# First attention's transposes into the second product's PSUM banks, and the second attention five pieces later

## The chip, the cores and the metric

The kernel runs on one core of a Trainium2 chip. The metric is the time of one execution on the device in microseconds (us); lower is better. Times are medians of several executions; a profile is one further execution with the hardware profiler on. The engines are PE (TensorE: matmuls and transposes), DVE (VectorE), ACT (ScalarE), POOL (GpSimd) and SP, whose queue issues nearly all DMAs. Each engine works through its own instructions in order.

## The reference

Attention with a causal window of 128 and a distance bias, then a two-layer product with the mish function, all in float32 (the two weight matrices arrive as float64):

```python
scores = q @ k.T / sqrt(64) + bias;  allowed where 0 <= i - j < 128   # batch 8, heads 8, seq 576, head 64
attn = softmax(scores);  x = attn @ v              # x becomes 4608 tokens x 512
h = x @ w_in                                       # 512 -> 2048
out = (h * tanh(softplus(h))) @ w_out              # 2048 -> 512
```

## The kernel before

The program is unrolled Python; every engine executes its instructions in program order, and that order is written out by hand: each piece of work is a pair (time, function), the lists are sorted by time (`run`, L536), and the numbers count units of attention or pieces of the product, not microseconds.

**Batches.** The 576 tokens of a batch are done as 512 and a remainder of 64; the remainders of all batches are the ninth round. Round `c` has a first product (`first`, L450: eight `j` of 24 matmuls) with `mish`, and a second product (`second`, L507: 32 pieces of six matmuls, number `2m + t`). While round `c` does its second product, the attention of batch `c + 1` is mixed into it. Attention of batch 0 has nothing to hide behind: it is the early stage, done with `attention(0, 0.27)` (L559).

**A unit of attention** (`unit`, L247) is two query blocks for a pair of heads; eight units `k` per batch, `p, half = divmod(k, 2)`. Its steps are: `scores` on PE into a PSUM tile `s` of two banks (two such tiles exist); `exps` (DVE takes bias and maximum, ACT the exponent); `fold` (POOL folds the exponents, DVE takes the reciprocals `r`, kept in the second bank of `s`); `scale` (DVE); `weights` (four PE transposes into the first bank of the same `s`, then one DVE multiplication by the masks back into `pz`); `values` (PE, into the one bank `o`); and for odd units `split_x` (ACT and DVE split `o` into a rounded and a remaining part, tile `x`). Even units also carry a `last_unit` (L356) for the 64 left-over tokens.

In the early stage `busy` (L549) adds two groups of four small matmuls per unit that write to unused columns of the second bank of `s` of the unit before: one group just after the next unit's scores, one just after the transposes.

**Converting the weights** (`convert_w`, L134). Each of the 16 weight pieces arrives as float64 bits in two halves and goes through `scaled` (ACT, to a temporary `t`), `joined` (three DVE bit operations, the first into a temporary `u`), `upper` (ACT) and `lower` (a subtraction). With `banks` given, `t` and `u` lie in PSUM banks and POOL does `lower`; with `None`, `t` is a slot of the SBUF ring `gg` (three slots, shared with `parts`), `u` is written over the input in SBUF, and DVE does `lower`. Pieces 0 and 1 are converted in the early stage, 2 to 11 during the first product of round 0, 12 to 15 (the last four of `w_out`, `Co4` to `Co7` below, needed from pieces 8, 10, 12 and 14 on) during the second product of round 0. The matmuls of the second product write to the banks `po0` and `po1`, which are unused in the early stage but for the first two conversions.

`parts` (L475) splits mish's result for the second product: ACT rounds, POOL subtracts, into a slot of `gg`; it runs two products `m` ahead.

Of the kernel before, what the change touches and what calls it, by code (L numbers as in the profile page):

```python
# [8 lines left out]
F32 = mybir.dt.float32  # L9
# [7 lines left out]
P = 128  # L17
# [18 lines left out]
def attention_mish_mlp(  # L36
# [35 lines left out]
    ps = ctx.enter_context(tc.tile_pool(name="ps", bufs=1, space=bass.MemoryType.PSUM))  # L72
# [17 lines left out]
    for t in vb:  # L90
# [3 lines left out]
    pe, dve, act, pool, sp = (  # L94
        InOrder(tc, e) for e in (nc.tensor, nc.vector, nc.scalar, nc.gpsimd, nc.sync)
    )
# [7 lines left out]
    def big(name, dtype):  # L104
        return wts.tile([P, 2048], dtype, tag="w", name=name, bufs=2 * NJ + NF // 4)
# [25 lines left out]
            else:  # L131
                load(t[:, :512].bitcast(F32).rearrange("p (c n) -> p c n", n=n), part)

    def convert_w(kind, j, banks):  # L134

        halves = raw_w.pop((kind, j))
        st = {}

        def value(a):
            return halves[a][:, 1::2].bitcast(F32) if bits else halves[a][:, :512].bitcast(F32)

        def place(a, part):
            return split[(kind, j)][:, 1024 * a + 512 * part : 1024 * a + 512 * part + 512]

        def scaled(a):  # L150
            if a == 0:
                split[(kind, j)] = big(f"s{kind}{j}", F32R)
            if not bits:
                return
            if banks:
                st[a] = ps.tile([P, 512], F32, tag=banks[a][0], name=f"t{kind}{j}_{a}")
            else:
                if a == 0:
                    st["t"] = ff.tile([P, 1024], F32, tag="gg", name=f"t{kind}{j}", bufs=3)
                st[a] = st["t"][:, 512 * a : 512 * (a + 1)]  # L160

            act.activation(st[a], value(a), AF.Copy, scale=2.0**-112)

        def joined(a):
            if not bits:
                return
            low, high, tb = halves[a][:, 0::2], halves[a][:, 1::2], st[a].bitcast(U32)
            u = high
            if banks:
                u = ps.tile([P, 512], F32, tag=banks[a][1], name=f"u{kind}{j}_{a}").bitcast(U32)  # L170
            dve.tensor_scalar(out=u, in0=tb, scalar1=3, scalar2=None, op0=ALU.logical_shift_left)
            dve.scalar_tensor_tensor(
                out=high, in0=low, scalar=29, in1=u, op0=ALU.logical_shift_right, op1=ALU.bitwise_or,
            )
            dve.scalar_tensor_tensor(
                out=high, in0=tb, scalar=0x80000000, in1=high, op0=ALU.bitwise_and,
                op1=ALU.bitwise_or,
            )

        def upper(a):  # L180
            act.activation(place(a, 0), value(a), AF.Copy)

        def lower(a):
            (pool if banks else dve).tensor_tensor(
                out=place(a, 1), in0=value(a), in1=place(a, 0).bitcast(F32), op=ALU.subtract
            )

        return scaled, joined, upper, lower
# [37 lines left out]
    def load_pair(b, p):  # L226
        hs = slice(2 * p, 2 * p + 2)
        qk = at.tile([P, 2, S], F32, tag="qk", name=f"qk{b}_{p}")
        load(qk[:, 0, :], qT[b, hs].rearrange("h d s -> (h d) s"))
        load(qk[:, 1, :], kT[b, hs].rearrange("h d s -> (h d) s"))  # L230
        z = qd[p % 2]
        for i in range(2):
            r = slice(i * D, (i + 1) * D)
            load(z[r, r], qT[b, 2 * p + i, :, CH:S])
        qkv[(b, p)] = (qk, z)
# [11 lines left out]
    def unit(b, p, half, lag):  # L247
# [6 lines left out]
        st = {}  # L254
        blocks = (0, 1) if half == 0 else (2, 3)
        name = f"{b}_{p}_{half}"
# [52 lines left out]

        def weights():  # L310
            pz = st["pz"]

            pt = st["s"][:, 0, :].rearrange("p (c n) -> p c n", c=4)
            for c in range(4):
                pe.transpose(pt[:, c, :], pz[:, c, :P], ident)
            dve.tensor_tensor(
                out=pz.rearrange("p c (u n) -> p u c n", u=2),
                in0=pt.rearrange("p (u c) n -> p u c n", u=1).to_broadcast([P, 2, 4, P]),
                in1=masks.rearrange("p u (c n) -> p u c n", c=1).to_broadcast([P, 2, 4, P]),
                op=ALU.mult,  # L320
            )
# [20 lines left out]
        def split_x():  # L342
# [7 lines left out]

        return [
            (0, scores), (0.02, lambda: exps(0)), (0.25, lambda: exps(1)), (0.7, fold), (0.95, scale),
            (1.3, weights), (1.99 + lag, values), (2.02 + lag, split_x),
        ]

    def last_unit(b, p, lag):  # L356
# [61 lines left out]
    def attention(b, lag=0.0):  # L418

        steps = []
        for k in range(2 * NP):
            p, half = divmod(k, 2)
            for u in [unit(b, p, half, lag)] + ([last_unit(b, p, lag)] if half == 0 else []):
                steps += [(k + d, f) for d, f in u]
            if half:
                nxt = (b, p + 2) if p + 2 < NP else (b + 1, p + 2 - NP)
                if 0 < nxt[0] < B:  # L430
                    steps.append((k + 0.03, lambda nxt=nxt: load_pair(*nxt)))
                    steps.append((k + 2.01, lambda nxt=nxt: load_v(*nxt)))
        return sorted(steps, key=lambda s: s[0])
# [16 lines left out]
    def first(c, j, blocks=range(NCC)):  # L450
        if blocks[0] == 0:
            hs[j % 2] = ps.tile([P, 2, CH], F32, tag="s", name=f"h{c}_{j}", bufs=2)
        h = hs[j % 2]
        for t, cc in (
            [(t, cc) for cc in blocks for t in range(2)] if len(blocks) < NCC
            else [(t, cc) for t in range(2) for cc in blocks]
        ):
            x = xt[(c, cc)]
            for k, (w_, x_) in enumerate(((0, 0), (0, 1), (1, 0))):
                pe.matmul(  # L460
                    h[:, t, :], lhsT=w_part("i", j, w_, cc)[:, t * P : (t + 1) * P],
                    rhs=x[:, x_, :], start=(cc == 0 and k == 0), stop=(cc == NCC - 1 and k == 2),
                )
# [20 lines left out]
    po = {}  # L484
# [51 lines left out]
    def run(steps):  # L536
        for _, work in sorted(steps, key=lambda s: s[0]):
            work()

    def converting(weights, times, banks):  # L540

        steps = []
        for (kind, j), at_ in zip(weights, times):
            st = []
            steps.append((at_[0], lambda kind=kind, j=j, st=st: st.extend(convert_w(kind, j, banks))))
            steps += [(t, lambda n=n, st=st: st[n // 2](n % 2)) for n, t in enumerate(at_)]
        return steps

    def busy(n, place):  # L549
        for _ in range(n):  # L550
# [6 lines left out]


    early = attention(0, 0.27) + converting(  # L559
        conv[:2],  # L560
        [
            (4.1, 4.6, 4.45, 4.97, 4.8, 5.3, 4.82, 5.32),
            (5.6, 6.1, 5.97, 6.45, 6.3, 6.8, 6.32, 6.82),
        ],
        (("po0", "po1"), ("po0", "po1")),
    )
    for k in range(2 * NP):
        if k:
# [2 lines left out]
    early += [  # L571
        (8.6, lambda: first(0, 0, (0,))),
        (9.3, lambda: first(0, 0, (1, 2))),
        (9.31, lambda: first(0, 0, (3,))),
    ]
    busy(18, ps.tile([P, 512], F32, tag="po0", name="idle")[:, : 2 * P])
    run(early)
# [1 line left out]
    for c in range(B + 1):  # L579

        steps = []
        for j in range(NJ):
            if c or j:
                steps.append((j, lambda j=j: first(c, j)))
            steps.append((j + 0.9, lambda j=j: mish(c, j)))
        steps += [(NJ - 1.05, lambda j=j: parts(c, 0, j)) for j in range(2)]
        if c == 0:
            steps += converting(
                conv[2:12],
                [  # L590
                    [-0.5 + 0.84 * n + d for d in (0, 0.42, 0.3, 0.72, 0.75, 1.15, 0.8, 1.2)]
                    for n in range(10)
                ],
                (("po0", "w"), ("po1", "o")),
            )
        run(steps)
        if c == 0:
            load_w(*last_w)

        n = 4 * NJ  # L600
        steps = []
        for m in range(2 * NJ):
            for t in range(2):
                steps.append((2 * m + t, lambda m=m, t=t: second(c, *divmod(m, NJ), t)))
            if m >= 2:
                steps.append((2 * m - 4.1, lambda m=m: parts(c, *divmod(m, NJ))))
        if c == 0:
            steps += converting(
                conv[12:],
                [  # L610
                    [0.3 + 2.5 * n + d for d in (0, 0.6, 0.8, 1.4, 1.7, 2.2, 2.0, 2.5)]
                    for n in range(4)
                ],
                None,
            )
        if c + 1 < B:
            steps += [((n - 2) / 9.0 * s - 0.2, f) for s, f in attention(c + 1)]
        elif c + 1 == B:
            steps.append((4.5, last_x))
        run(steps)  # L620
# [63 lines left out]
```

## Time and profile before

| | us |
|---|---|
| median of 3 runs | 1052.24 (1049.55 to 1052.77) |
| profiled execution | 1053.68 |
| its span, first to last instruction | 1051.9 |
| mean granted TensorE clock | 0.982 of full speed |
| PE busy in the span | 1008.9 (96%) |
| DVE, ACT, POOL busy | 367.1, 395.6, 293.4 |

The profiled execution lies 1.78 us above its span and 1.44 us above the median. Busy PE time counts matmuls at either clock, so a full row of PE is not yet PE at its best; the stages have to be looked at one by one.

### The profile page before, as it was taken

What the parts mean: (1) busy time and instruction counts of PE and PEld (TensorE: products, weight loads), DVE (VectorE), ACT (ScalarE), POOL (GpSimd) and SP (SyncE); (2) the same over time, 40 slices, a digit from 0 to 9 for tenths busy, and PEclk for the clock granted to TensorE, in tenths of its full rate; (3) what the DMA queues carried; (4) which work ended last, traced back from release to release, by engine and by line L of the source; (5) the groups of instructions that cost most, each with busy time, mean ns of one, the idle gap of its engine ahead of it and who ended that gap; (6) DMA issues with size and microseconds to landing.
All of it is one profiled execution on the core that took longest, in us unless ns stands there. A gap on an engine that the chain in (4) does not pass through costs nothing.

```text
span 1051.9 us, 14258 instructions
## 1 busy us (share of the span) xinstructions
PE 1008.9 (96%) x5358; PEld 793.8 (75%) x5358; DVE 367.1 (35%) x1118; ACT 395.6 (38%) x958; POOL 293.4 (28%) x286
## 2 busy tenths in 40 slices
PE   7579969999999999999999999999999999999998
PEld 4348747787778877887788777877787778888886
DVE  4659796402550065005520463026401650010000
ACT  3437744314442354225421543145324542231121
POOL 2215633203330244004410432033302440141042
PEclk9869988999999999999999999999999999999999
DMA  8940111200220023002210032003100201010001
GB/s 271 398 173 1 64 37 57 69 1 25 72 61 30 1 62 93 33 1 61 68 59 1 26 94 68 1 26 93 55 15 5 69 24 41 1 41 21 1 0 41
DMA packets 52133, 59.32 MB, mean 56 GB/s; under 512 B 13024, under 2 KB 32608, under 8 KB 52064
## 3 DMA queue, kind: packets, MB, share of 16 engines
q1 hardware_dynamic: 50880, 57.69, 17.1%
q8 instruction: 42, 0.69, 0.3%
q10 hardware_dynamic: 1184, 0.72, 0.2%
q14 instruction: 27, 0.22, 0.1%
HBM read 47.91 MB, written 10.49 MB: 56 GB/s over the span
## 4 chain that ended last, share of the span: by engine, by line
PE 88%; DVE 3%; ACT 1%; issue 1%; POOL 1%; ACTq 0%; DVEq 0%; POOLq 0%
PE h L30 37%; PE po L30 37%; PE s L30 9%; PE o L30 5%; DVE wo L30 1%; DVE pz L30 1%; ACT pz L30 0%; POOL gg L30 0%; PE pt_3l L30 0%; ACT so L30 0%; DVE so L30 0%; POOL so L30 0%; PE pt_2l L30 0%; PE pt_1l L30 0%; ACT gg L30 0%
## 5 line engine op out<-in xcount | busy, mean ns | idle before, releaser
L30 PE MATMUL po<-so,gg 128*128 128x512 f32 x1728 | 433.2, 401 | 0.0
L30 PE MATMUL h<-x,si 128*128 128x512 f32 x1728 | 394.6, 390 | 0.0
L30 PEld LDWEIGHTS h<-x,si 128*128 128x128 f32 x1728 | 325.0, 188 | 67.7 <-issue 0.2
L30 POOL TENSOR_TENSOR gg<-g,gg 128x512 fp32r<-128x512 f32 x144 | 185.8, 1294 | 671.9 <-ACT gg L30 570.3
L30 PEld LDWEIGHTS po<-so,gg 128*128 128x128 f32 x1728 | 317.6, 190 | 73.3 <-issue 5.7
L30 DVE CUSTOM_DVE_ANT_0 pz<-s,nb 128x256 f32<-128x256 f32 (+1 forms) x256 | 84.6, 387 | 300.9 <-PE s L30 300.8
L30 ACT ACTIVATE g<-h 128x1024 f32<-128x1024 f32 x72 | 73.9, 1027 | 269.1 <-PE h L30 269.1
L30 ACT ACTIVATE pz<-pz,mx 128x256 f32<-128x256 f32 (+1 forms) x256 | 120.4, 471 | 138.4 <-DVE mx L30 138.4
L30 ACT ACTIVATE gg<-g 128x512 fp32r<-128x512 f32 x144 | 88.5, 621 | 48.2 <-PE po L30 46.7
L30 DVE TENSOR_TENSOR pz<-s,masks 128x1024 f32<-128x1024 f32 x64 | 78.2, 1222 | 23.8 <-PE s L30 23.8
L30 POOL TENSOR_TENSOR pz<-pz 128x256 f32<-128x256 f32 x64 | 65.6, 1025 | 29.4 <-ACT pz L30 19.2
L30 DVE TENSOR_TENSOR pz<-pz,s 128x512 f32<-128x512 f32 x64 | 43.8, 684 | 83.9 <-POOL pz L30 83.5
L30 PE MATMUL s<-qk 64*128 64x128 f32 (+1 forms) x448 | 57.7, 376 | 0.0
L30 PE MATMUL o<-pz,va 128*64 128x128 f32 (+1 forms) x560 | 54.9, 325 | 1.6 <-DVE pz L30 1.5
L30 PEld LDWEIGHTS o<-pz,va 128*64 128x64 f32 x560 | 33.3, 136 | 29.7 <-issue 12.0
L30 DVE COPY ob<-po 128x512 f32<-128x512 f32 x18 | 12.4, 691 | 117.4 <-PE po L30 117.4
L30 PE MATMUL s<-ident,pz 128*128 128x128 f32 x256 | 41.2, 286 | 10.6 <-DVE pz L30 9.2
L30 ACT ACTIVATION_READ_ACCUMULATOR pz<-pz,mx 128x1 f32 x256 | 47.8, 187 | 0.0
L30 PEld LDWEIGHTS s<-ident,pz 128*128 128x128 f32 x256 | 32.4, 146 | 20.2 <-DVE pz L30 6.0
L30 ACT ACTIVATE x<-o 128x512 fp32r<-128x512 f32 x32 | 18.8, 587 | 65.0 <-PE o L30 64.6
L30 DVE TENSOR_TENSOR x<-o,x 128x512 fp32r<-128x512 f32 x32 | 22.1, 692 | 59.0 <-ACT x L30 59.0
L30 PEld LDWEIGHTS s<-qk 64*128 64x128 f32 x448 | 33.9, 186 | 11.2 <-issue 8.2
(117 smaller groups left out, 471.8 us busy)
## 6 DMA issues: line engine op xcount, KB each, us to landing
wi<-in_moe_w_in_dram SPq DMA_DIRECT2D x16, 512.0 KB, 10.6
wo<-in_moe_w_out_dram SPq DMA_DIRECT2D x16, 512.0 KB, 10.2
out_dram<-ob SPq DMA_DIRECT2D x32, 256.0 KB, 2.0
qk<-in_q_dram SPq DMA_DIRECT2D x28, 288.0 KB, 3.5
qk<-in_k_dram SPq DMA_DIRECT2D x28, 288.0 KB, 3.8
va<-in_v_dram SPq DMA_DIRECT2D x28, 256.0 KB, 2.8
first<-in_q_dram SPq DMA_DIRECT2D x4, 288.0 KB, 3.8
first<-in_k_dram SPq DMA_DIRECT2D x4, 288.0 KB, 4.3
```

What stands on the lines that cost most here:

```text
L30: return self.tc.keep_in_program_order(method(*args, **kwargs))
```

## The change

- In batch 0, the four transposes of a unit go to a tile in bank `po0` or `po1` (by `half`) instead of the unit's own `s`.
- The first two conversions, which had these banks, use the SBUF ring `gg` instead (with `None`), start one unit earlier, and keep POOL for `lower` (a new argument `last` names that engine).
- `split_x` of batch 0 moves from unit time 2.29 to 2.45, that is from ahead of the masks' multiplication to behind it; the last part of the first product of round 0 moves from 9.31 to 9.5, behind it.
- In the second product of round 0, the four conversions start 0.6 of a piece earlier and follow each other every 2.0 pieces instead of 2.5; the attention of batch 1 begins five pieces later and takes 25/9 pieces a unit instead of 30/9, so that it ends at the same piece. Later rounds keep their times.

```diff
-    def convert_w(kind, j, banks):
+    def convert_w(kind, j, banks, last=pool):
...
         def lower(a):
-            (pool if banks else dve).tensor_tensor(
+            last.tensor_tensor(
                 out=place(a, 1), in0=value(a), in1=place(a, 0).bitcast(F32), op=ALU.subtract
             )
...
         def weights():
             pz = st["pz"]
-
-            pt = st["s"][:, 0, :].rearrange("p (c n) -> p c n", c=4)
+            if b == 0:
+                pt = ps.tile([P, 4, P], F32, tag=f"po{half}", name=f"pt{name}")
+            else:
+
+                pt = st["s"][:, 0, :].rearrange("p (c n) -> p c n", c=4)
             for c in range(4):
                 pe.transpose(pt[:, c, :], pz[:, c, :P], ident)
...
-            (1.3, weights), (1.99 + lag, values), (2.02 + lag, split_x),
+            (1.3, weights), (1.99 + lag, values), (2.45 if lag else 2.02, split_x),
...
-    def converting(weights, times, banks):
+    def converting(weights, times, banks, last=pool):
...
-            (4.1, 4.6, 4.45, 4.97, 4.8, 5.3, 4.82, 5.32),
-            (5.6, 6.1, 5.97, 6.45, 6.3, 6.8, 6.32, 6.82),
+            (3.1, 3.6, 3.47, 3.97, 3.8, 4.3, 3.82, 4.32),
+            (4.6, 5.1, 4.97, 5.47, 5.3, 5.8, 5.32, 5.82),
         ],
-        (("po0", "po1"), ("po0", "po1")),
+        None, pool,
     )
...
-        (9.31, lambda: first(0, 0, (3,))),
+        (9.5, lambda: first(0, 0, (3,))),
...
-                    [0.3 + 2.5 * n + d for d in (0, 0.6, 0.8, 1.4, 1.7, 2.2, 2.0, 2.5)]
+                    [-0.3 + 2.0 * n + d for d in (0, 0.4, 0.7, 1.5, 1.5, 2.4, 1.9, 2.6)]
                     for n in range(4)
                 ],
-                None,
+                None, dve,
             )
         if c + 1 < B:
-            steps += [((n - 2) / 9.0 * s - 0.2, f) for s, f in attention(c + 1)]
+
+            t0 = 0 if c else 5
+            steps += [(t0 + (n - 2 - t0) / 9.0 * s - 0.2, f) for s, f in attention(c + 1)]
```

## Rows read from the trace of the kernel before

**Rows 1.** The page's slices of PE: busy tenths in 40 slices of the span.

```profile
PE   7579969999999999999999999999999999999998
```

**Rows 2.** Windows (early stage; second product, round 0): length, busy by engine, clock, DMA.

```profile
7.00:81.00 74.00, 51.21 (x312) 35.23 (x313) 45.90 (x141) 27.49 (x92) 14.20 (x16) 0.84 0.78 278
119.20:205.70 86.50, 73.88 (x421) 55.33 (x421) 61.55 (x162) 42.38 (x115) 34.02 (x30) 0.92 0.21 63
```

**Rows 3.** Waits of PE from 9.8 to 75 us: total, times, longest.

```profile
PE s L30 <- DVE pz L30: 22.5, 11, 4.6
```

**Rows 4.** Timeline of PE, early stage: start, length, instruction [idle before, releaser].

```profile
24.21 0.60 PE L30 MATMUL s<-masks 128*128 128x256 bf16 x4 [1.32 <-DVE pz L30]
26.57 1.09 PE L30 MATMUL o<-pz,first 128*64 128x128 f32 x12
27.59 0.66 PE L30 MATMUL s<-ident,pz 128*128 128x128 f32 x4
...
30.97 1.00 PE L30 MATMUL s<-masks 128*128 128x256 bf16 x4 [2.73 <-DVE pz L30]
...
48.82 1.01 PE L30 MATMUL s<-masks 128*128 128x256 bf16 x4 [4.64 <-DVE pz L30]
...
75.77 1.09 PE L30 MATMUL o<-pz,first 128*64 128x128 f32 x12
```

**Rows 5.** Timeline of DVE, early stage: masks' multiplication of unit 1, scales of units 1, 2, 3, 7.

```profile
18.96 0.69 DVE L30 TENSOR_TENSOR pz<-pz,s 128x512 f32<-128x512 f32 x1
22.93 1.23 DVE L30 TENSOR_TENSOR pz<-s,masks 128x1024 f32<-128x1024 f32 x1 [0.35 <-PE s L30]
25.32 0.67 DVE L30 TENSOR_TENSOR pz<-pz,s 128x512 f32<-128x512 f32 x1
...
33.05 0.69 DVE L30 TENSOR_TENSOR pz<-pz,s 128x512 f32<-128x512 f32 x1
...
69.12 0.69 DVE L30 TENSOR_TENSOR pz<-pz,s 128x512 f32<-128x512 f32 x1
```

**Rows 6.** Lines by form, DVE, 10 to 73 us: busy, mean ns; a joining operation with PSUM temporaries.

```profile
L30 DVE SCALAR_TENSOR_TENSOR wi<-wi,ui 128x512 uint32<-128x512 uint32 x4 | 2.8, 688 | 0.1
```

**Rows 7.** The weight load that is issued fourth (piece 1, second half), and its landing.

```profile
L30 SPq DMA_DIRECT2D wi<-in_moe_w_in_dram x1: 467/467/467, 18.2 to 18.2; - x1
...
DMA to landing us min/median/max: 8.1/8.1/8.1
```

**Rows 8.** Timeline of PE, second product of round 0.

```profile
134.46 1.11 PE L30 MATMUL s<-ident,pz 128*128 128x128 f32 x4 [5.56 <-DVE pz L30]
135.44 5.22 PE L30 MATMUL po<-so,gg 128*128 128x512 f32 x12
...
146.97 3.00 PE L30 MATMUL po<-so,gg 128*128 128x512 f32 x12
```

**Rows 9.** Lines by form, DVE, 119 to 166 us: busy, mean ns | idle before.

```profile
L30 DVE SCALAR_TENSOR_TENSOR wo<-to,wo 128x512 uint32<-128x512 uint32 x10 | 8.3, 830 | 0.3
L30 DVE TENSOR_TENSOR so<-wo,so 128x512 fp32r<-128x512 f32 x8 | 8.0, 1020 | 2.6 <-ACT so L30 2.6
L30 DVE SCALAR_TENSOR_TENSOR wo<-wo 128x512 uint32<-128x512 uint32 x8 | 6.5, 816 | 0.3
L30 DVE CUSTOM_DVE_ANT_0 pz<-s,nb 128x256 f32<-128x256 f32 x12 | 4.6, 418 | 0.0
L30 DVE TENSOR_SCALAR wo<-to 128x512 uint32<-128x512 uint32 x8 | 4.3, 532 | 3.7 <-ACT to L30 3.7
```

**Rows 10.** Timeline, second product of round 0: ACT's last `upper` of `Co3`; DVE's longest joining.

```profile
122.19 0.66 ACT L30 ACTIVATE so<-wo 128x512 fp32r<-128x512 f32 x1
...
153.02 1.66 DVE L30 SCALAR_TENSOR_TENSOR wo<-wo 128x512 uint32<-128x512 uint32 x1
```

**Rows 11.** Timeline of PE: second product of round 1 begins, and the next first product.

```profile
249.34 0.93 PE L30 MATMUL s<-qk 64*128 64x128 f32 x8
...
316.96 8.32 PE L30 MATMUL h<-x,si 128*128 128x512 f32 x36
```

More of the change, by code (lines that the diff above doesn't have):

```diff
@@ L544, in converting @@
             st = []
-            steps.append((at_[0], lambda kind=kind, j=j, st=st: st.extend(convert_w(kind, j, banks))))
+            steps.append((at_[0], lambda kind=kind, j=j, st=st: st.extend(convert_w(kind, j, banks, last))))
             steps += [(t, lambda n=n, st=st: st[n // 2](n % 2)) for n, t in enumerate(at_)]
```

## The prediction

> **What bounds the kernel now.** I read the page's slices first, 40 of 26.3 us each: PE stands at 9 or more tenths from the seventh slice to the last but one [rows 1], so PE bounds the kernel there, and what does not let PE run sooner or denser elsewhere is worth nothing. The lean slices are the first three and the sixth, the two stretches that the change touches. The windows give their sizes [rows 2]. In the early stage PE is busy 51.2 of 74 us at a granted clock of 0.84; in the second product of round 0 it is busy 73.9 of 86.5 at 0.92. The same second product in round 1, with the same attention but no conversions, takes 316.96 - 249.34 = 67.6 us [rows 11]. So 18.9 us are at stake there, and about 23 of idle in the early stage. Between the two lies the first product of round 0, from the values of unit 7 at 75.77 [rows 4] to 119.2; PE is dense there and the change only shifts it.
>
> In the early stage all of PE's large waits are for DVE: 22.5 us in eleven waits [rows 3]. The timeline tells them apart [rows 4]. Three stand before the first `busy` group of a unit, which needs the reciprocals read by `scale`. Eight stand before the second group, behind the transposes: 1.32 at 24.21 (five such), 2.73 at 30.97, 4.64 at 48.82, one of 2.50. They end when DVE's multiplication by the masks ends: 22.93 + 1.23 = 24.16 [rows 5]. It reads the transposes out of the very `s` that `busy` writes, and the next scores of that `s` stand behind. That is a loop through PE and DVE, once per unit.
>
> In the second product the largest wait, 5.56 us, is that of the transposes of unit 0 for `scale` at 134.46 [rows 8]; DVE is full with conversions there.
>
> **The change, part by part.** *Transposes in `po0`/`po1`.* The eight waits for the masks leave their place. PE goes on to the next scores and next waits for `scale`. How long a unit then takes: from the end of one `scale`, PE does `busy` 0.60, values 1.09, transposes 0.66 [rows 4], DVE the masks 1.23, and then the small work up to the end of the next `scale`, 25.99 - 24.16 = 1.83 [rows 5]: 5.4 us. The scores and exponents of the next unit fit beside this, since the scores are now ahead of it. The other half of a pair has the subtraction of `split_x` where this one has the left-over unit's score; I take the same 5.4. Before, the six units from the end of scale 1 (19.65) to that of scale 7 (69.81) took 50.2 [rows 5]. After: 6 x 5.4 = 32.4, plus the four halves of conversions, which lie in the loop: with SBUF temporaries the means are 0.532 + 0.816 + 0.830 = 2.18 each [rows 9], 8.7 together, against 3 x 0.69 = 2.1 with PSUM ones [rows 6]. Then the clock. Rows 4 show `busy` at 0.60 at full rate (24.21), but 1.00 and 1.01 (1.2 instead of 2.4 GHz) after PE had idled 2.73 and 4.64. Where a conversion lengthens a unit, PE still idles that long for `scale`; at the ratio 1.01/0.60 the 2.35 us of PE in a unit become 4.0. Bounds: no unit slowed, 0; all six, 9.9. I take three, the ones with most conversion: 5.0. Together 46.1 instead of 50.2: -4.1. Ahead of it the first wait of this kind, 1.3, is gone, and behind it the last, 1.3 (the matmuls of the first product then wait for nothing). Early stage: -6.7, between -1.8 and -11.7.
>
> *Conversions a unit earlier.* ACT asks for piece 0 at about 25 us instead of 36. The fourth load lands at 18.2 + 8.1 = 26.3 [rows 7], and piece 1 is asked for a unit and a half later: no wait. POOL's subtractions keep their count.
>
> *`split_x` behind the masks.* Nothing, as PE needs the masks first and `o` is written again only a unit later; without that cover it would be its 0.69 in a pair. The moved quarter of the first product follows it and is in order.
>
> *Second attention five pieces later.* It issues the same instructions. Its load of the pair after next moves with it on SP, behind the last halves of the weights, which it does not pass; it is needed three units later, so it is hidden. The table load before the first exponent no longer stands ahead of `Co4`, while nothing else of ACT is late for it. What counts is when `scale` of unit 0 is done, since PE's transposes wait for it and all pieces stand behind them. PE reaches them after nine pieces at 1.5 (3.00 for two [rows 8]) and three groups of scores near 0.9 [rows 11]: 119.2 + 16.2 = 135.4. DVE has, ahead of that `scale`, all joinings and three weights' subtractions. It begins when ACT has left `Co3` (122.85 [rows 10]) and scaled one half, 123.5; eight halves x 2.18 = 17.4, six subtractions x 1.02 = 6.1, four exponents' maxima at 0.42 at most, 1.4, and the small work 1.83 up to `scale` [rows 5, 9]: 150.2. So PE stands for some 15 us in one wait, where before it stood in several. Behind it lie 67.6 - 16.2 = 51.4 of dense PE [rows 11]. To this come the clock after the idling, as before (5.22 against 3.00 for two pieces [rows 8]), 2.2, and smaller waits. Those were 86.5 - 73.9 - 5.6 = 7.0 [rows 2, 8]; the conversions are gone by then, so I take half, 3.5, with 0 and 7 as ends. End: 207.3 instead of 205.7, +1.6.
>
> Joining with both operands in SBUF: Rows 6 show 0.688 with the temporary in PSUM, rows 9 means of 0.816 and 0.830 with it in SBUF, and rows 10 one of 1.66. The Trainium skill ("SBUF — State Buffer", section "Who interferes with whom") says that a DVE instruction with two SBUF inputs and a POOL instruction that reads SBUF exclude each other, the later one blocking fully; the stretched rows agree. By it alone, each joining that meets POOL would pay like the longest row, which is the third rival below; by the means the sum stands.
>
> **Sum.** -6.7 + 1.6 = -5.1. On the profiled execution, 1053.7, that is 1048.6; the median lies 1.4 below it, so 1047.
>
> **Rivals.**
> *Clock stays low.* All six early units run at 1.2 GHz, because `busy` does not fill the waits for `scale`: the early stage gives only 1.8. For it: 0.84 of the clock over the stage. Against: the waits that went were the ones before the slow rows. -1.8 + 1.6: 1052, no change. The change then does nothing that can be seen, though the waits moved.
> *Second product gains too.* POOL has fewer instructions beside the conversions once the attention is late. Joinings at 3 x 0.69 and subtractions at 0.69 give 123.5 + 16.5 + 4.1 + 3.2 = 147.3; without small waits and slow clock the end is 198.7, -7.0, together -13.7: 1038.5. The true case may lie part of the way.
> *DVE holds the second attention back (slower).* If every two-operand joining is as long as the longest, 1.66, a half costs 3.85, `scale` of unit 0 ends at 123.5 + 30.8 + 9.3 = 163.6, the stage at 220.7, +15: together +8.3, 1060.5. The change is even when that `scale` ends at 155.3, and slower by 0.3% from 158.5 on. Against: only one joining in eight halves was that long.
>
> **How the numbers follow.** This kernel's runs spread by 0.3%, about 3.2 us, which is what can be told from no change. Forecast 0.62 (1042 to 1051: early -4 to -9, second -3 to +5); low clock 0.18; second product gains 0.12; slower 0.08. Faster by over 0.3% (below 1049): most of the forecast, 0.54, the gaining case 0.12, and a little of the low clock: 0.69. Within: 0.22. Slower: 0.09. The range from 1040.5 to 1052.5 leaves out the slower case, half of the gaining one and the edges.
>
> **What would show it.** In the early stage PE's waits before `s<-masks` are only those for `scale`, and no `busy` group starts at the end of a masks' multiplication; scale 1 to scale 7 in 44 to 48 us; the first product of round 0 shifted earlier by 5 to 9. In round 0's second product: no idle PE in the first nine pieces beyond small ones, one wait of 12 to 16 us before the first transposes, and the next first product 85 to 91 us after the first piece. Wrong if `busy` still waits for the masks, if ACT waits for a weight or for a slot of `gg`, or if `scale` of unit 0 ends more than 37 us after the stage's start (155.3 - 119.2 = 36.1).

## The result and the profile after

The changed kernel takes 1045.44 us (median of 5 runs, 1043.91 to 1047.03) against 1052.24 for the kernel before in the same series (1049.55 to 1053.75). The ratio is 0.9938, with a 95% interval of 0.9924 to 0.9952: by the ratio, 6.5 us or 0.6% faster. The profiled execution took 1047.03, with a span of 1045.3.

The two windows of [rows 2], cut at the same events, come first. The columns are length, busy time by engine, granted clock and DMA.

```profile
7.00:71.30 64.30, 47.39 (x313) 33.48 (x314) 46.21 (x141) 27.95 (x92) 14.43 (x16) 0.84 0.91 320
109.60:199.10 89.50, 71.06 (x421) 52.35 (x422) 61.09 (x161) 42.33 (x115) 31.96 (x30) 0.92 0.19 61
```

The early stage is 9.7 us shorter than in [rows 2], at the same mean clock. The second product is 3.0 us longer. PE has the same instructions and 3.8 and 2.8 us less busy time in the two stages, so fewer of them ran at the low clock. The mean clock counts PE's idle time too: from 134 to 139 us, where PE does nothing, it reads 0.50.

PE's waits in the early stage, to be laid beside [rows 3], and the rows of PE's timeline that answer to [rows 4]:

```profile
PE s L30 <- DVE pz L30: 15.0, 6, 4.9
PE o L30 <- issue: 1.7, 1, 1.7
```

```profile
66.04 1.09 PE L30 MATMUL o<-pz,first 128*64 128x128 f32 x12
```

Eleven waits of 22.5 us have become six of 15.0, and each of the six ends with a `scale`; no `busy` group starts at the end of a multiplication by the masks any more. The values of unit 7 start at 66.04 instead of 75.77.

What the second `busy` group held up shows in DVE's rows of a left-over unit, first before and then after the change. In PE's queue the left-over unit's transpose stood behind `busy`, and DVE, with its next `scale` still to come, waited 1.3 us for it, in each of the four even units. That wait is gone.

```profile
32.22 0.42 DVE L30 TENSOR_TENSOR pf_1l<-pt_1l,masks 128x256 f32<-128x256 f32 x1 [1.31 <-PE pt_1l L30]
```

```profile
26.70 0.41 DVE L30 TENSOR_TENSOR pf_1l<-pt_1l,masks 128x256 f32<-128x256 f32 x1
```

DVE's rows for [rows 5], the scales of units 1, 2 and 3 and those of 4 to 7:

```profile
17.20 0.69 DVE L30 TENSOR_TENSOR pz<-pz,s 128x512 f32<-128x512 f32 x1 [0.69 <-POOL pz L30]
...
22.59 0.67 DVE L30 TENSOR_TENSOR pz<-pz,s 128x512 f32<-128x512 f32 x1
...
29.90 0.69 DVE L30 TENSOR_TENSOR pz<-pz,s 128x512 f32<-128x512 f32 x1
...
38.06 0.69 DVE L30 TENSOR_TENSOR pz<-pz,s 128x512 f32<-128x512 f32 x1 [1.13 <-POOL pz L30]
...
48.56 0.69 DVE L30 TENSOR_TENSOR pz<-pz,s 128x512 f32<-128x512 f32 x1
...
55.69 0.67 DVE L30 TENSOR_TENSOR pz<-pz,s 128x512 f32<-128x512 f32 x1
...
61.21 0.69 DVE L30 TENSOR_TENSOR pz<-pz,s 128x512 f32<-128x512 f32 x1
```

From scale to scale that is 5.4, 7.3, 8.2, 10.5, 7.1 and 5.5 us, 44.0 in all. The two units without conversions or cold clock, the first and the last, take 5.4 and 5.5; the prediction built 5.4 from single rows.

In the second product, PE's timeline (for [rows 8]):

```profile
109.65 1.62 PE L30 MATMUL po<-so,gg 128*128 128x512 f32 x6
111.61 5.74 PE L30 MATMUL po<-so,gg 128*128 128x512 f32 x24 [0.34 <-DVE wo L30]
...
125.37 1.19 PE L30 MATMUL po<-so,gg 128*128 128x512 f32 x4 [1.03 <-ACT gg L30]
127.05 0.73 PE L30 MATMUL po<-so,gg 128*128 128x512 f32 x2 [0.49 <-POOL gg L30]
141.40 1.09 PE L30 MATMUL s<-ident,pz 128*128 128x128 f32 x4 [13.61 <-DVE pz L30]
...
199.07 1.29 PE L30 MATMUL h<-x,si 128*128 128x512 f32 x5
```

One wait of 13.61 us has taken the place of the several of before. What DVE did up to it shows in its groups from 109.6 to 150 us, which answer to [rows 9], and in four rows of its timeline: the first operation of `Co4`, two subtractions of the conversions that wait for ACT, and the `scale` of unit 0.

```profile
L30 DVE TENSOR_TENSOR so<-wo,so 128x512 fp32r<-128x512 f32 x8 | 8.3, 1036 | 3.6 <-ACT so L30 3.5
L30 DVE SCALAR_TENSOR_TENSOR wo<-wo 128x512 uint32<-128x512 uint32 x8 | 6.5, 815 | 0.3
L30 DVE SCALAR_TENSOR_TENSOR wo<-to,wo 128x512 uint32<-128x512 uint32 x9 | 6.2, 693 | 0.3
L30 DVE TENSOR_SCALAR wo<-to 128x512 uint32<-128x512 uint32 x8 | 4.6, 569 | 2.1 <-ACT to L30 2.1
```

```profile
113.70 1.09 DVE L30 TENSOR_SCALAR wo<-to 128x512 uint32<-128x512 uint32 x1 [2.14 <-ACT to L30]
...
120.32 1.34 DVE L30 TENSOR_TENSOR so<-wo,so 128x512 fp32r<-128x512 f32 x1 [0.71 <-ACT so L30]
...
134.67 1.32 DVE L30 TENSOR_TENSOR so<-wo,so 128x512 fp32r<-128x512 f32 x1 [1.55 <-ACT so L30]
...
140.58 0.67 DVE L30 TENSOR_TENSOR pz<-pz,s 128x512 f32<-128x512 f32 x1
```

### The profile page after: what moved, and what is told of

Same layout as the page of the kernel before. It is cut to its first block, busy times and chain, and to the rows that moved or that the text cites. A ratio compares the mean times of both kernels' runs of the same rounds, so it can differ in the third digit from the quotient of the medians.

```text
span 1045.3 us, 14263 instructions
## 1 busy us (share of the span) xinstructions
PE 1002.5 (96%) x5358; PEld 789.3 (76%) x5358; DVE 367.0 (35%) x1118; ACT 395.9 (38%) x958; POOL 292.0 (28%) x286
## 4 chain that ended last, share of the span: by engine, by line
PE 83%; DVE 1%; ACT 1%; POOL 0%; issue 0%; POOLq 0%
PE po L30 36%; PE h L30 33%; PE s L30 8%; PE o L30 4%; DVE pz L30 0%; POOL gg L30 0%; PE pt_1l L30 0%; PE pt_2l L30 0%; PE pt_3l L30 0%; PE pt_0l L30 0%; ACT pz L30 0%; POOL pz L30 0%; ACT gg L30 0%; ACT x L30 0%; ACT pz_3l L30 0%
## 5 line engine op out<-in xcount | busy, mean ns | idle before, releaser
L30 DVE TENSOR_TENSOR pz<-s,masks 128x1024 f32<-128x1024 f32 x56 | 68.5, 1223 | 21.1 <-PE s L30 21.1
L30 PE MATMUL s<-qk 64*128 64x128 f32 (+1 forms) x448 | 57.7, 376 | 0.0
L30 PE MATMUL s<-ident,pz 128*128 128x128 f32 x224 | 34.1, 275 | 15.5 <-DVE pz L30 14.4
L30 PEld LDWEIGHTS s<-ident,pz 128*128 128x128 f32 x224 | 27.8, 141 | 23.5 <-ACT pz_0l L30 14.0
L30 ACT ACTIVATE x<-o 128x512 fp32r<-128x512 f32 x32 | 18.8, 588 | 61.6 <-PE o L30 61.2
## 6 DMA issues: line engine op xcount, KB each, us to landing
wo<-in_moe_w_out_dram SPq DMA_DIRECT2D x16, 512.0 KB, 10.5
```

The lines of the kernel that those rows point to most:

```text
L30: return self.tc.keep_in_program_order(method(*args, **kwargs))
```

## The experiments

All ratios are to the kernel before, run on the same chip in the same series; its medians there were 1051.71 to 1052.24. "Second product" is the length of that stage in the run's profile, from its first matmul to the next first product. Single profiles differ for two reasons that no edit explains. The first `scale`, which comes behind the first loads, began at 11.5 to 13.0 us. And eight kernels have the changed early stage in full (the changed kernel, e1, e4 and e7 to e11): in the profiles of two, the changed kernel and e8, PE is at the low clock behind scale 7, and the values of unit 7 begin 4.1 us after the end of that `scale`; in the other six they begin after 2.5. The transposes of unit 7 and the `busy` group behind them, in the changed kernel and in e1:

```profile
62.04 0.92 PE L30 MATMUL pt<-ident,pz 128*128 128x128 f32 x4
62.76 1.06 PE L30 MATMUL s<-masks 128*128 128x256 bf16 x4
```

```profile
60.88 0.63 PE L30 MATMUL pt<-ident,pz 128*128 128x128 f32 x4
61.35 0.60 PE L30 MATMUL s<-masks 128*128 128x256 bf16 x4
```

So gains are taken from medians and stages from profiles; kernels with the old second product show 86.5 to 88.0 us there, which is how far a stage's length can be trusted.

| kernel | median us | ratio (95%) | second product us |
|---|---|---|---|
| before | 1052.24 | 1 | 86.5 |
| changed | 1045.44 | 0.9938 (0.9924 to 0.9952) | 89.4 |
| e1 early part only | 1042.57 | 0.9908 (0.9893 to 0.9923) | 88.0 |
| e2 second part only | 1053.97 | 1.0025 (1.0015 to 1.0035) | 89.4 |
| e3 `busy` elsewhere | 1043.54 | 0.9912 (0.9897 to 0.9927) | 87.9 |
| e4 `lower` on POOL | 1045.97 | 0.9942 (0.9928 to 0.9956) | 90.9 |
| e5 before, no second `busy` | 1046.50 | 0.9951 (0.9939 to 0.9964) | 86.5 |
| e6 old early conversions | 1042.09 | 0.9916 (0.9902 to 0.9929) | 86.5 |
| e7 delay 12 | 1036.89 | 0.9862 (0.9849 to 0.9875) | 81.5 |
| e8 delay 0, new times | 1046.50 | 0.9951 (0.9938 to 0.9964) | 90.2 |
| e9 delay 5, old times | 1044.90 | 0.9932 (0.9917 to 0.9948) | 87.7 |
| e10 delay 12, old times | 1037.59 | 0.9861 (0.9844 to 0.9879) | 81.6 |
| e11 delay 16 | 1043.68 | 0.9918 (0.9903 to 0.9934) | 88.0 |
| e12 e1, no second `busy` | 1045.55 | 0.9940 (0.9925 to 0.9955) | 86.9 |

**e1 and e2: one part at a time.** To the changed kernel (e1), and to the kernel before (e2):

```diff
# e1: the second product's times of before
-   [-0.3 + 2.0 * n + d for d in (0, 0.4, 0.7, 1.5, 1.5, 2.4, 1.9, 2.6)]
+   [0.3 + 2.5 * n + d for d in (0, 0.6, 0.8, 1.4, 1.7, 2.2, 2.0, 2.5)]
-   t0 = 0 if c else 5
+   t0 = 0
# e2: the reverse of these lines, in the kernel before
```

> The early part of the change alone; the second product of round 0 keeps its times of before. Theory: the two parts add up, the early one gives about 9.7 us (first values of unit 7 at 66.0 instead of 75.8 us) and the second one costs about 3 us (the stage from its first matmul to the next first product takes 89.4 us in the changed kernel and 86.5 in the kernel before). Then this run takes 1052.2 - 9.7 = 1042.5 us, about 3 us less than the changed kernel, and its second product takes 86 to 87 us. Rival: the second part is needed, because a first product that ends earlier meets conversions and loads that come no earlier; then the second product takes 89 us or more here too, and the run takes 1045 us or more.

> The second part of the change alone (conversions and second attention of round 0 at their new times); the early stage as before. Theory: the parts add up, so this run is slower than before by about 3 us, 1055 us, with its second product at about 89 us and the transposes of its first unit 31 to 32 us after the stage's start. Rival: the second part is free or helps by itself, 1052 us or less, and the longer stage of the changed kernel comes from its earlier start.

Both came out as the theory had them: the early part alone gains 0.92% (9.7 us, interval 8.1 to 11.3), the second part alone loses 0.25% (2.6 us, interval 1.6 to 3.7). The sum, 7.1, is the changed kernel's 6.5 within the error. In e2's profile the single wait before the first transposes is again 13.61 us, after an early stage as slow as before (scale 1 to scale 7 in 50.0 us), so the earlier start has no part in it.

**e3: what closes the loop.**

```diff
# on top of e1
-   if b == 0:  pt = ps.tile(..., tag=f"po{half}")
+   (transposes of batch 0 in s again)
-   early.append((k + 1.35, lambda k=k: busy(4, places[0, k][:, 1, 256:])))
+   early.append((k + 1.35, lambda: busy(4, idle[:, : 2 * P])))   # a tile in po0
```

> The early part alone with one edit taken back: the transposes of batch 0 stand in s again, and the second busy group of each unit writes to an unused bank (po0) instead of s. Theory: the loop through PE and DVE was closed by the second busy group, so moving that group away gives the whole early gain: 1042.5 us, equal to the run with the early part alone. Rival: the transposes' bank closes it, because the scores two units later write the same s and wait for the masks too; then a wait of PE for the masks comes back in front of the scores, unit for unit, and the run takes 1048 to 1052 us.

The time is that of e1, 0.9912 against 0.9908. So it was the second `busy` group that closed the loop; with that group out of the way, the bank of the transposes makes no difference here. The rival saw a real wait, though. PE's waits and three rows of its timeline:

```profile
PE s L30 <- DVE pz L30: 18.1, 12, 4.7
```

```profile
34.68 1.14 PE L30 MATMUL s<-first 64*128 64x256 f32 x8 [1.07 <-DVE pz L30]
37.74 0.60 PE L30 MATMUL s<-masks 128*128 128x256 bf16 x4 [1.92 <-DVE pz L30]
...
42.05 1.54 PE L30 MATMUL s<-first 64*128 64x128 f32 x12 [1.56 <-DVE pz L30]
```

The scores do wait for the masks, by 1.07 and 1.56 us, twelve waits of 18.1 us where e1 has six of 14.6. They cost nothing: scale 1 to scale 7 takes 44.0 us in both, since the next `scale` ends later anyhow. Only a wait in front of the *next* link of the chain counts, and `busy` stood there: ahead of the left-over unit's transpose, for which DVE waited.

**e5 and e12: the second `busy` group left out**, once from the kernel before and once from e1; what it writes is never read.

```diff
-   early.append((k + 1.35, lambda k=k: busy(4, places[0, k][:, 1, 256:])))
```

> The kernel before without the second busy group of each unit (the one behind the transposes); all else as before. Those matmuls write nothing that is read. Theory: that group closes the loop, so leaving it out takes PE's waits for the masks away and gives a good part of the early gain even at a lower granted clock: 1043 to 1048 us, the span from scale 1 to scale 7 at 44 to 47 us instead of 50. Rival: the group earns its place by keeping the granted clock up; without it the matmuls of the units run at 1.2 GHz and the run takes 1052 us or more.

> The early part of the change alone, without the second busy group of each unit (its matmuls write nothing that is read). Theory: the group no longer stands in front of anything, it only keeps PE active; without it the granted clock falls in more units and the run takes 1044 to 1047 us. Rival: the group is worth nothing any more, since PE's idle stretches all stand before scale, ahead of the other group: 1042 to 1043 us.

Both theories held in the time. In the kernel before, leaving the group out gains 5.2 us (0.49%), and scale 1 to scale 7 falls from 50.2 to 47.3, just outside the 44 to 47 expected. But PE's waits for the masks did not go away, as had been expected too: they moved to the scores, and with those for `scale` PE has ten of them. Its waits in e5 and one of the rows:

```profile
PE s L30 <- DVE pz L30: 19.6, 10, 3.5
```

```profile
16.03 2.75 PE L30 MATMUL s<-first 64*128 64x128 f32 x12 [1.10 <-DVE pz L30]
```

These scores run cold and end at 18.8, a microsecond after scale 1 (17.8), and the unit that follows takes 7.1 us; in e12, with the transposes in the other bank, it takes 5.4. So where PE is cold, a wait in front of the scores can cost something, unlike in e3.

In e1, where it waits for nothing, leaving it out loses some 3.4 us (0.9940 against 0.9908). The granted clock from 10 to 66 us shows why, first e12 and then e1:

```profile
10.00:66.00 56.00, 36.83 (x237) 25.02 (x236) 42.18 (x133) 25.63 (x87) 14.41 (x16) 0.76 0.97 347
```

```profile
10.00:66.00 56.00, 40.00 (x282) 28.13 (x281) 42.41 (x127) 25.94 (x86) 14.43 (x16) 0.82 0.97 348
```

The group keeps the clock up (0.82 against 0.76), and before the change its place in the queue cost more than that was worth. What e12 has over e5 is all the rest of the early part together (the bank, the conversions, the moved `split_x`): 46.3 us from scale 1 to scale 7 instead of 47.3, with ratios whose intervals overlap. Against e1, e12 takes 2.3 us more from scale 1 to scale 7, and all of it in two units: the interval from scale 2 to 3 is 8.4 instead of 7.3, that from 6 to 7 is 6.7 instead of 5.5. The intervals from 3 to 6 are the same to 0.1 us, cold or not.

**e6: the early conversions at their old times**, on top of e1:

```diff
-   (3.1, 3.6, 3.47, 3.97, 3.8, 4.3, 3.82, 4.32),
-   (4.6, 5.1, 4.97, 5.47, 5.3, 5.8, 5.32, 5.82),
+   (4.1, 4.6, 4.45, 4.97, 4.8, 5.3, 4.82, 5.32),
+   (5.6, 6.1, 5.97, 6.45, 6.3, 6.8, 6.32, 6.82),
```

> The early part alone (second product as before) with the two early conversions put back to their old times, one unit later. Theory: the conversions lengthen whichever unit they fall into, so their place is worth nothing in the loop, but the last ones now fall behind unit 6: 1042.5 to 1044 us. Rival: the earlier place is a part of the gain (the units without conversions must be the last ones for the clock to stay up in the first product's beginning): 1045 us or more.

No difference from e1 (0.9916 and 0.9908, intervals overlapping): the conversions lengthen whichever units they fall into, as the theory said. Scale 1 to scale 7 takes 44.8 us, and the longest unit, 10.4, is now that from scale 5 to scale 6.

**e4: `lower` of `Co4` to `Co7` on POOL**, in the changed kernel:

```diff
-   None, dve,
+   None, pool,
```

> The changed kernel with the last subtraction of the conversions of Co4 to Co7 on POOL instead of DVE. Theory: the wait of 13.6 us before the first transposes of the second attention is the sum of what DVE has ahead of that scale; without the six subtractions of 1.02 us it ends about 6 us earlier, PE's wait falls to some 7 us, and the run takes 1038 to 1041 us. Rival: DVE and POOL hold each other up where both read SBUF, so DVE's joinings become as much longer, or POOL's own queue (the split of mish's result) comes late; then the scale comes no earlier and the run takes 1045 us or more.

The rival held. DVE lost the subtractions, and yet the `scale` of unit 0 ended 32.7 us after the stage's start instead of 31.6. DVE's groups from 106.9 to 139 us, and rows of DVE and of POOL at one moment:

```profile
L30 DVE SCALAR_TENSOR_TENSOR wo<-to,wo 128x512 uint32<-128x512 uint32 x9 | 12.0, 1339 | 0.3
L30 DVE SCALAR_TENSOR_TENSOR wo<-wo 128x512 uint32<-128x512 uint32 x8 | 6.9, 866 | 0.3
L30 DVE TENSOR_SCALAR wo<-to 128x512 uint32<-128x512 uint32 x8 | 6.6, 829 | 3.2 <-ACT to L30 3.2
```

```profile
114.87 0.69 DVE L30 SCALAR_TENSOR_TENSOR wo<-wo 128x512 uint32<-128x512 uint32 x1
115.60 1.68 DVE L30 SCALAR_TENSOR_TENSOR wo<-to,wo 128x512 uint32<-128x512 uint32 x1
```

```profile
115.36 1.37 POOL L30 TENSOR_TENSOR so<-wo,so 128x512 fp32r<-128x512 f32 x1 [2.13 <-ACT so L30]
...
119.45 1.75 POOL L30 TENSOR_TENSOR so<-wo,so 128x512 fp32r<-128x512 f32 x1
```

A joining is 0.69 us alone and 1.64 to 1.68 where it begins beside one of POOL's subtractions; six of the nine second joinings did, three of them beside a moved subtraction and three beside the split of mish's result, which the changed kernel has as well. The three kinds of joining operation together grew by 9 x 0.646 + 8 x 0.051 + 8 x 0.260 = 8.3 us, more than the six subtractions that `scale` had had ahead of it (6.4). The Trainium skill ("SBUF — State Buffer", section "Who interferes with whom") says that a DVE instruction with two SBUF inputs contends with a POOL instruction that reads SBUF, over a pair of ports that only one of them can hold, and the rows agree. Work moved from DVE to POOL bought no time here, because the joinings paid for it.

**e7, e10 and e11: the attention later still; e8 and e9: the two edits of the second part apart.** In the changed kernel (e10 and e9 with the old conversion times as well, as in e1):

```diff
-   t0 = 0 if c else 5
+   t0 = 0 if c else 12      # e7, e10;  16 in e11;  5 in e9;  t0 = 0 in e8
```

> The changed kernel with the second attention beginning twelve pieces later instead of five. Theory: PE stands because its queue holds the first transposes after nine pieces while DVE still converts; with four to five more pieces ahead of the transposes PE waits for the weights Co5, Co6 and Co7 instead, by some 3 us each at 10, 12 and 14 pieces, in all about 9 us in place of 15.5, so the second product takes 80 to 84 us and the run 1037 to 1041 us. Rival: the attention has too few pieces left to hide behind; its units become bound by their own chain and waits for the masks come back at the end of the stage: 1045 us or more.

> The changed kernel with the second attention not delayed, the four conversions at their new, denser times. Theory: it is the delay of the attention that costs the 3 us, so this run takes 1041 to 1043.5 us. Rival: the denser conversions cost it, since DVE does them ahead of the attention's steps: 1045 us or more.

> The changed kernel (attention delayed by five pieces) with the four conversions of the second product back at their old times. Together with the runs of the early part alone (attention at 0, old times), the run without delay (0, new times) and the changed kernel (5, new times) it fills a table of two by two. Theory, after the run without delay came out as slow as the changed kernel: the denser conversions cost the 3 us and the delay by five pieces costs nothing, so this run takes 1041 to 1043.5 us. Rival: each of the two costs by itself, because a delay to the middle of the stage gathers the waits into one: 1045 us or more.

> Attention delayed by twelve pieces with the conversions at their old times. Theory: with the attention behind them, all conversions stand together on DVE whatever their times, so the run equals that with the new times, 1036 to 1038.5 us, or gains a little from it. Rival: the old times are the better ones here too, by the same 3 us: 1034 us or less; or the old times are too late for the pieces now that PE meets them earlier: 1040 us or more.

> The changed kernel with the second attention delayed by sixteen pieces. A unit then has 14/9 pieces, 2.3 us of product and about 3.3 us of its own matmuls, 5.6 us, about the 5.4 us of a unit's own chain. Theory: the 1.9 us that PE still waits before the first transposes with twelve pieces vanish, the rest holds: 1034 to 1037 us. Rival: without reserve the units become bound by their chain, PE waits for scale or masks in several units at 1 us or more each: 1039 us or more.

With twelve pieces of delay the kernel takes 1036.89 us, 1.4% faster than before, and beats the changed kernel and e1. PE's timeline of e7:

```profile
107.10 1.63 PE L30 MATMUL po<-so,gg 128*128 128x512 f32 x6
...
117.22 1.20 PE L30 MATMUL po<-so,gg 128*128 128x512 f32 x4 [1.06 <-ACT gg L30]
...
122.78 1.20 PE L30 MATMUL po<-so,gg 128*128 128x512 f32 x4 [2.09 <-ACT gg L30]
...
128.65 1.49 PE L30 MATMUL po<-so,gg 128*128 128x512 f32 x4 [2.08 <-ACT gg L30]
...
142.38 0.63 PE L30 MATMUL s<-ident,pz 128*128 128x128 f32 x4 [1.91 <-DVE pz L30]
...
188.60 13.76 PE L30 MATMUL h<-x,si 128*128 128x512 f32 x60
```

The theory had the sum (8.3 us of waits, the four here and four under 0.5; 9 expected) and the stage (81.5; 80 to 84 expected), but it named the wrong releaser: by the profile PE does not wait for the weights, it waits for the split of mish's result. ACT's rows show where that stands:

```profile
120.96 0.69 ACT L30 ACTIVATE so<-wo 128x512 fp32r<-128x512 f32 x1 [2.68 <-DVE wo L30]
121.54 0.67 ACT L30 ACTIVATE to<-wo 128x512 f32<-128x512 f32 x1
122.10 0.63 ACT L30 ACTIVATE gg<-g 128x512 fp32r<-128x512 f32 x1
```

In ACT's queue the rounding of `gg` stands behind an `upper`, and that waits 2.68 us for DVE's joining. It is DVE's fullness all the same, reaching PE by way of ACT.

With sixteen pieces (e11) the rival held: the first waits are those of e7, but then units wait for `scale`, masks and left-over units, nine times between 0.17 and 2.12 us (three of them above 1), and the stage is 88.0 long. e10 equals e7, so behind the conversions their spacing no longer matters.

The table of e1, e8, e9 and the changed kernel is less clear. The new times without delay (e8) are as slow as the changed kernel, so the denser conversions cost what was lost: 3.9 us by the medians of e1 and e8, 2.3 by their stages. With 1044.9 us e9 falls between its theory and its rival. By its stage, 87.7 us, among those of the old second product, it says that the delay by five costs nothing; by its median it is 2.3 us slower than e1 and only 0.5 faster than the changed kernel. The two profiles, e9's and e1's, differ by 1.5 us in their spans, and that is the first `scale`, which ends at 13.7 us instead of 12.2; from there on they agree in every stage to 0.3 us. So no stage shows a cost of the delay by five with the old times; how much of the 2.3 us between the medians is the delay's stays open.

## Why the prediction was right, and where it was off

It said 1047 with a range from 1040.5 to 1052.5, and faster with 0.69; the median is 1045.4. Both mechanisms were right, and both terms too small in size: -6.7 and +1.6 were foreseen, -9.7 and about +2.6 to +3.2 came (e1; e2, and e1 to the changed kernel). The two errors, 3.0 and 1.0 to 1.6, have opposite signs, so the total came out nearer than its parts; that is luck.

**Early stage.** The eight waits for the masks left, as predicted, and e3 and e5 show that `busy` behind the transposes had closed the loop. The prediction had only the next scores behind that group; the left-over unit's transpose, for which DVE waited, stood there too. The chain unit of 5.4 us was right to 0.1. Of the bounds of the forecast, "scale 1 to scale 7 in 44 to 48" held at its edge (44.0), "shifted earlier by 5 to 9" did not (9.7 in this profile; 12.5 in e1's, 1.4 of it the earlier first `scale`). Against the sum: the six units took 44.0 instead of 46.1 (-6.2 against -4.1); ahead of scale 1 it gave 1.8 instead of 1.3 (0.3 of it because the first `scale` came earlier in this profile); behind scale 7, 1.8 instead of 1.3, and 3.4 in the six profiles in which the clock stayed up there. In the six units, conversions and clock together had 8.7 + 5.0 = 13.7 and measured 44.0 - 32.4 = 11.6. The twelve operations that DVE does for the four halves add up to 9.2 in the changed kernel's timeline, so the term that was mis-sized is the clock: if the conversions lie in the chain in full, as the sum had them, at most 2.4 is left for it instead of 5.0.

Three units ran cold, as guessed (in e1 `busy` takes 0.76, 1.01 and 1.01 us after scales 3, 4 and 5), but only one paid for it. The unit from scale 5 to 6, cold and without conversions, takes 7.1, that is 1.7 over the 5.4, where the sum had 1.65 for a cold unit: in it DVE stood 1.91 and 0.81 us for PE's results. The other two have conversions as well, and there the two terms were added though they hide each other. The unit from scale 3 to 4 takes 2.8 over the 5.4, and its conversion half alone is 2.7. After scale 4 PE is cold in e1 and warm in e3 (0.60 at 37.74 above), and the unit takes 10.5 us in both. DVE and ACT set its length: in ACT's queue the rounding of `o` stands behind four exponents and two steps of a conversion, and DVE's subtraction of `split_x` waits for it, e1 first and then e3:

```profile
43.46 0.69 DVE L30 TENSOR_TENSOR x<-o,x 128x512 fp32r<-128x512 f32 x1 [0.26 <-ACT x L30]
```

```profile
43.56 0.69 DVE L30 TENSOR_TENSOR x<-o,x 128x512 fp32r<-128x512 f32 x1 [1.24 <-ACT x L30]
```

In e1 DVE had already stood 0.88 us for the cold transposes, and that came off its wait for ACT. Behind it the second conversion half follows, with a joining of 1.63, ahead of the next `scale`. That a cold clock costs only where DVE waits for PE last, e12 says from the other side.

The rival of a clock that stays low gave 1052. The mean clock did stay low (0.84, as before), and the gain came nonetheless: a mean clock over a stage says nothing on whether PE's rows were on the chain.

**Second product.** Step by step: DVE began `Co4` 4.05 us after the stage's start (4.3 predicted); `scale` of unit 0 ended at 31.6 (31.0), with the joinings a little cheaper than thought (2.08 a half against 2.18) and 2.3 us of waits of DVE for ACT that the sum did not have, so that its nearness is in part two errors that cancel; PE waited 13.61 (about 15, in "12 to 16"); from there to the end it took 57.7 (57.1). The stage is 89.4 long instead of 88.1, inside "85 to 91". One statement failed: PE was not free of waits in the first nine pieces but stood three times, 1.86 us. It cost nothing, because the `scale` behind came later still. The slower rival, with each joining at 1.66, did not occur in the changed kernel: one of sixteen was that long. In e4 it came about in part, with seven of sixteen, for the reason given there, and cancelled what the move should have gained.

**Conversions a unit earlier, `split_x`, loads.** Costed at nothing. For the conversions e6 bears it out. In the early stage ACT waited for no weight and for no slot of `gg`, and in the second product no engine waited for a load. The moved `split_x` did show: the wait of 1.7 us whose releaser the profile does not name is that of the values of unit 6, and it ends with the subtraction. In e1 that is at 59.65, and `scale` of unit 7, which PE needs next, ends at 60.74, so most of the wait lies beside DVE's work. The move was not tried alone; together with the bank and the conversions it is in the difference between e5 and e12.

What the prediction did not ask is whether five pieces was enough. Its own sum had PE at the transposes 15 us ahead of `scale`; with that much idle left, the attention belonged further behind the conversions, and e7 is another 0.8% faster (0.9862 against 0.9938).

## What to carry to other kernels

A filler matmul is in the queue like any other: write it to a tile that nobody else touches, since one that shares a tile with live data takes over its waits, and can cost more than the clock it holds: here it was worth 3.4 us where it waited for nothing, and leaving it out gained 5.2 where it waited. When work is put later so that a full engine gets through first, work out when that engine is done and put it there: half the way gathered several waits into one of 13.6 us, the whole way left 1.9 of it, and too far left the chain of the late work bare. Terms for two causes in the same unit are not to be added before it is asked which engine ends that unit last.

## What the runs showed of the hardware

Only POOL's side of the hold-up was not expected: in e4 its own 128x512 subtractions also rose, from 1.30 to 1.75 us, where they met DVE's joinings, and DVE's one-operand shift was stretched as well, from 0.42 to between 1.09 and 1.54 us. And PE's `busy` group of four showed 0.76 and 0.71 us at single places in e1, between 0.60 at the full clock and 1.01 at half of it: a group can lie across a change of the granted clock, which over these two reads 0.69 and 0.85. Nor is the clock the same in every execution: with the same instructions up to there, and the same wait of PE of 1.7 us before the values of unit 6, two of eight profiles had it low behind scale 7, which cost 1.6 us, and six did not.
